# A 32-group attention with an FFN behind it on one core: other filler products on TensorE, later loads for the last batch, and a new table of priorities

## The chip, the cores and the metric

One core of one Trainium2 chip runs the kernel. The metric is the device time of one execution in microseconds; lower is better. TensorE (PE; its weight loads are listed as PEld), VectorE (DVE), ScalarE (ACT), GpSimd (POOL) and SyncE (SP) each work through a list of instructions of their own, in order, and wait for each other through semaphores. POOL and SP also issue the transfers (DMA).

## The reference

Block-sorted attention, and behind it a feed-forward network with a leaky activation:

```python
# q, k, v: (4, 8, 768, 64); sort_net: (4, 8, 8, 8)
for _ in range(5):                          # Sinkhorn
    P = P - max(P, -1); P = exp(P)
    P = P / (sum(P, -1) + 1e-9)
    P = P / (sum(P, -2) + 1e-9)
k_sorted = einsum('bhij,bhjcd->bhicd', P, k_b)   # 8 blocks of 96 rows
v_sorted = einsum('bhij,bhjcd->bhicd', P, v_b)
attn = softmax(q_b @ k_sb.T / sqrt(64))          # inside each block of 96
x = (attn @ v_sb) -> (3072, 512)
h = x @ w_in                                     # 512 -> 2048
out = (max(h, 0) + alpha * min(h, 0)) @ w_out    # 2048 -> 512, float32
```

## The kernel before

The work is cut into 32 groups: group g is block g % 8 of batch g // 8, 96 rows of all 8 heads. `attention(g)` makes the scores (`psS`), their row maximum on VectorE, the exponentials on ScalarE, the product with v (`psO`) and the normalised result `xq`; from group 8 on the weights (`ET`) and the result (`xT`) are turned by DMA transposes that SP issues, before that on TensorE. `ffn1` (line 820) multiplies 2 or 4 groups with 128 columns of w_in into `psH`, and ScalarE (`t`) and VectorE (`hT`) apply the activation; `ffn2` (line 852) multiplies 128 rows with w_out into `psYP` and writes them out.

Ahead of a batch's attention its inputs are prepared. For batch 0 the q loaded at line 423 is turned by `prep_q` (identity products, line 615), k is sorted by `prep_k` (line 615), v is copied into another layout by `conv_v` (ACT, DVE or POOL, line 671) and sorted by `prep_v` (line 682). For batches 2 and 3, `conv_k` (DVE, `KZ<-KS`) and `conv_v` (POOL, 16 copies) lay the data out first, and q comes as eight loads `QN` that six DMA transposes `QTz<-QN` (`turn_q`, line 433) turn; each of these needs all eight loads.

The loads of batch 3 are held back by `paced(g, n)` (line 418): load number n waits for the ET transpose (n even) or the xT transpose (n odd) of group g + n // 2. v starts at g = 9 (line 464), k at 11 (line 452), q at 13 (line 430, two heads for each n).

Every operation is added to a graph with a duration, keys that it reads and writes, and a priority. `plan` (line 205) adds to each priority a shift that two characters of the table `ORDER` give, up to 41 either way (a group counts 1), and `schedule` (line 156) runs the graph in a model of the engines: the operation that can start first goes, by priority among those ready within 60 ns. The result is a fixed list for each engine. In the model, `span` (line 118) counts TensorE's instructions, two for each product, and lets TensorE wait where a count of 256 more is passed sooner than `FETCH_NS` after the last such point (2,500 ns after 36 us); `FETCH0` (line 31) gives the count, the time of the last point and the next threshold to begin with.

`fill` (line 214) then puts extra products into TensorE's list, whose results nobody reads, wherever the model leaves a gap before the first FFN steps. The list begins with 96 products of 16 columns (`short`, line 1006) as soon as the identity matrix is there. A gap that begins before 9 us in the model is filled with bf16 identity products of 512 columns, priced 480 ns each; a later one first with f32 identity products of 512 columns (865 ns) and then with bf16 ones (216 ns), to 0.9 of its length (`warm`, line 998).

## Time and profile before

| | us |
|---|---|
| median of 3 runs | 250.53 (248.55 to 250.69) |
| profiled execution | 250.59 |
| its span, first to last instruction | 248.9 |
| TensorE busy in the span | 231.8 |
| VectorE busy | 177.1 |
| ScalarE busy | 152.2 |
| GpSimd busy | 85.5 |

The profile is one execution. Busy time is the time in which an engine has at least one instruction running; the chain of waits goes back from the last instruction to what released each step. A row of the timeline has start, length, engine, line, operation, output and inputs with their shape, count, and in brackets the idle time before it and what ended it. "issue" is time for which the profile shows no cause.

### The profile page before, as it was taken

The numbers are of one execution on the slowest core, as the hardware profiler recorded it, in microseconds if no ns is written. First come the engines' busy times: TensorE is split into PE (matmuls) and PEld (weight loads), VectorE is DVE, ScalarE is ACT, GpSimd is POOL, SyncE is SP. The second block draws the span as 40 slices with busy tenths as digits, with TensorE's granted clock in tenths as the row PEclk, the third lists the DMA queues.
The fourth block names the chain that finished last, engine by engine and source line by source line (L and its number), as shares of the span: only waits on it lengthen the run. The fifth ranks groups of instructions, "written<-read, shape, count | busy, mean of one in ns | idle before, by whom it ended". The sixth has DMA issues, their size and how long they took to land.

```text
span 248.9 us, 6237 instructions
## 1 busy us (share of the span) xinstructions
PE 231.8 (93%) x2548; PEld 136.3 (55%) x2548; DVE 177.1 (71%) x357; ACT 152.2 (61%) x419; POOL 85.5 (34%) x105
## 2 busy tenths in 40 slices
PE   3997899989889997997999999999999999999995
PEld 3655467667545554554555555555555455555553
DVE  5875497887998969499875668967767877354430
ACT  5564455587966787365875587565775674453441
POOL 8969970089999238995000000000000000000000
PEclk9997999999999999999999999999999999999999
DMA  5999999999699999998445236453334342110112
GB/s 104 202 188 210 208 208 174 210 209 148 82 147 157 185 157 157 161 138 126 34 116 123 37 86 121 84 105 91 87 79 112 60 106 72 47 42 0 43 63 109
DMA packets 66941, 29.79 MB, mean 120 GB/s; under 512 B 58704, under 2 KB 61536, under 8 KB 66912
## 3 DMA queue, kind: packets, MB, share of 16 engines
q0 software_dynamic: 24256, 13.63, 41.0%
q1 hardware_dynamic: 42656, 15.76, 33.9%
q8 instruction: 20, 0.33, 0.5%
q14 instruction: 9, 0.07, 0.1%
HBM read 27.28 MB, written 6.29 MB: 135 GB/s over the span
## 4 chain that ended last, share of the span: by engine, by line
PE 69%; DMA 11%; DVE 8%; POOL 7%; issue 3%; ACT 2%; POOLq 0%; DVEq 0%; SPq 0%
PE psH L830 26%; PE psYP L869 25%; DMA ET<-Esb 6%; DMA VST<-in_v_dram 5%; PE psS L869 3%; PE psO L783 3%; POOL QN L427 3%; POOL VD L397 2%; PE psS L728 2%; DVE KZ L397 2%; DVE hT L843 2%; PE psS L740 1%; DVE xq L793 1%; PE psO L682 1%; DVE nm L734 1%
## 5 line engine op out<-in xcount | busy, mean ns | idle before, releaser
L843 DVE SCALAR_TENSOR_TENSOR hT<-t,omaT,psH 128x384 bf16<-128x384 f32 (+1 forms) x139 | 77.2, 570 | 38.0 <-ACT t L840 36.6
L830 PE MATMUL psH<-xT,w_in_bf 128*128 128x384 bf16 (+1 forms) x556 | 96.9, 311 | 2.9 <-DVE hT L843 2.9
L840 ACT ACTIVATE t<-psH 128x384 f32<-128x384 f32 (+1 forms) x139 | 62.9, 465 | 52.4 <-PE psH L830 47.3
L869 PE MATMUL psYP<-w_out_bf,hT 128*128 128x512 bf16 x336 | 84.6, 379 | 0.0
L830 PEld LDWEIGHTS psH<-xT,w_in_bf 128*128 128x128 bf16 x556 | 49.8, 98 | 36.0 <-DVE hT L843 7.7
L761 ACT ACTIVATE Esb<-psS,nf 96x96 bf16<-96x96 f32 x192 | 46.3, 345 | 1.8 <-DVE nf L734 1.6
L869 PEld LDWEIGHTS psYP<-w_out_bf,hT 128*128 128x128 bf16 x336 | 30.2, 98 | 28.0 <-DVE outstg L397 0.2
L397 POOL COPY VD<-VST 64x384 bf16<-64x384 bf16 (+1 forms) x39 | 34.8, 893 | 19.3 <-DMA VST<-in_v_dram 16.5
L734 DVE TENSOR_REDUCE nf<-psS 96x8 f32<-96x768 f32 x24 | 22.7, 948 | 0.9 <-PE psS L728 0.9
L793 DVE TENSOR_TENSOR xq<-psO,rec 96x512 bf16<-96x512 f32 x31 | 21.2, 685 | 0.9
L427 POOL DMA_DIRECT2D QN<-in_q_dram x24 | 20.7, 877 | 0.0
L397 ACT ACTIVATE VS<-psYP 112x512 bf16<-112x512 f32 x16 | 11.0, 687 | 4.1 <-PE psYP L690 2.7
L790 DVE RECIPROCAL rec<-psO 96x8 f32<-96x8 f32 x31 | 6.2, 200 | 8.3 <-PE psO L783 8.3
L783 PEld LDWEIGHTS psO<-VS,ET 112*128 112x128 bf16 x192 | 8.6, 98 | 6.0 <-DMA ET<-Esb 2.6
L783 PE MATMUL psO<-VS,ET 112*128 112x65 bf16 x192 | 9.9, 194 | 1.6 <-DMA ET<-Esb 1.5
L728 PE MATMUL psS<-KT,QTz 64*128 64x96 bf16 x248 | 10.8, 207 | 0.3 <-ACT Esb L761 0.3
L397 ACT ACTIVATE KT<-psYP 128x512 bf16<-128x512 f32 x11 | 6.6, 597 | 7.2 <-PE psYP L643 4.6
L397 ACT ACTIVATE outstg<-psYP 128x512 f32<-128x512 f32 x12 | 7.2, 597 | 5.7 <-PE psYP L869 5.7
L728 PEld LDWEIGHTS psS<-KT,QTz 64*128 64x128 bf16 x248 | 6.3, 95 | 7.7 <-ACT t L840 3.6
L869 PE MATMUL psS<-w_out_bf,hT 128*128 128x512 bf16 (+1 forms) x48 | 9.3, 344 | 0.0
L397 DVE COPY KZ<-KS 64x1024 bf16<-64x1024 bf16 x12 | 8.4, 710 | 0.1
L397 DVE CAST VS<-psYP 112x512 bf16<-112x512 f32 x10 | 6.8, 683 | 2.3 <-PE psYP L690 2.3
(140 smaller groups left out, 210.1 us busy)
## 6 DMA issues: line engine op xcount, KB each, us to landing
out_dram<-outstg SPq DMA_DIRECT2D x23, 256.0 KB, 2.4
QN<-in_q_dram POOLq DMA_DIRECT2D x24, 96.0 KB, 4.8
w_in_bf<-in_moe_w_in_dram POOLq DMA_DIRECT2D x8, 256.0 KB, 15.9
w_out_bf<-in_moe_w_out_dram POOLq DMA_DIRECT2D x2, 1024.0 KB, 26.4
VST<-in_v_dram POOLq DMA_DIRECT2D x4, 384.0 KB, 19.3
KS<-in_k_dram POOLq DMA_DIRECT2D x2, 768.0 KB, 28.4
KZ<-in_q_dram POOLq DMA_DIRECT2D x1, 768.0 KB, 6.5
KS<-in_k_dram POOLq DMA_DIRECT2D x2, 384.0 KB, 8.8
```

The source lines that it names most:

```text
L397: return e.activation(o, i, ACTF.Copy) if e is nc.scalar else e.tensor_copy(o, i)
L427: G.add(POOL, lambda e, h=h: e.dma_start(AP(QN, h % 4 * 128 + (h // 4) * 64, [[3072, 128], [512, 6], [1, 64]]), AP(q.tensor, b * HB + h * ...
L728: inst = e.matmul(o, AP(QTz[n], hp * 64 * QP + h4 * 768 + i * 96, [[QP, 64], [1, 128]]), AP(KT[n], hp * 64 * ld + (h4 * 8 + i) * bk, [[ld, ...
L734: G.add(DVE, lambda e: e.tensor_reduce(AP(nx, 0, [[8, 96], [4, 2], [1, 4]]), AP(psX, 0, [[1024, 96], [512, 2], [96, 4], [1, 96]]), AxisLis ...
L761: inst = e.activation(AP(Esb[me], p * 128, [[1024, 96], [64, 2], [1, 48]]), AP(psX, (p // 4) * 512 + (p % 4) * 96, [[1024, 96], [48, 2], [ ...
L783: inst = e.matmul(AP(psZ, hp * 512 + h4 * 68, [[1024, 128], [1, 65]]), AP(ET[me] if far else Es0[m], pos(h4, hp) * 96, [[800, nk], [1, 128]]),
L790: G.add(DVE, lambda e: e.reciprocal(AP(rec[m], 0, [[8, 96], [4, 2], [1, 4]]), AP(psZ, 64, [[1024, 96], [512, 2], [68, 4]])), 200, r=banks_ ...
L793: G.add(DVE, lambda e: e.tensor_tensor(out=AP(xq[me], 0, [[512, 96], [256, 2], [64, 4], [1, 64]]), in0=AP(psZ, 0, [[1024, 96], [512, 2], [ ...
L830: inst = e.matmul(AP(pt, poff, [[1024, 128], [1, n]]), AP(w_in_bf, kt * DFF + ft * 128, [[KT_TILES * DFF, 128], [1, 128]]), AP(xT, kt * XR ...
L840: G.add(ACT, lambda e: e.activation(AP(t1[tb], 0, [[384, 128], [1, n]]), AP(pt, poff, [[1024, 128], [1, n]]), ACTF.Relu, scale=-1.0), t_ac ...
L843: G.add(DVE, lambda e: e.scalar_tensor_tensor(out=AP(hT, ft * RING + tok % RING, [[FT_TILES * RING, 128], [1, n]]), in0=AP(t1[tb], 0, [[38 ...
L869: inst = e.matmul(AP(bank[0], bank[1], [[1024, 128], [1, n]]), AP(hT, ft * RING + tok % RING, [[FT_TILES * RING, 128], [1, 128]]), AP(w_ou ...
```

## The change

- The 96 short products are gone. Gaps are filled with bf16 identity products of 512 columns alone, priced 430 ns where the gap begins before 6 us in the model and 216 ns later. The first gap now begins with the identity matrix.
- The loads of batch 3 wait for groups five later: v from group 14, k from 16, q from 18.
- In the planner, `FETCH_NS` is 6000 for 5500, `FETCH0` is (70, -9000, 193) for (205, 6100, 449), and `conv_v` of batches 0 and 1 is priced 580 ns on DVE and 1000 on POOL, for 530 and 870.
- `ORDER` is another table of the same length. The operations and their dependencies are otherwise the same.

```diff
-FETCH_NS = 5500
-FETCH0 = (205, 6100.0, 449)
+FETCH_NS = 6000
+FETCH0 = (70, -9000.0, 193)
 ORDER = (
...
-    def fill(self, make, head, spans):
-
-        out, last = [head], 0.0
-        head.idx = len(self.ops)
-        self.ops.append(head)
+    def fill(self, make, spans):
+
+        out, last = [], 0.0
         for op in self.order["pe"]:
             for lo, hi, deps, bank in spans:
                 begin = max([last, lo] + [self.ops[d].end + 300 for d in deps])
-                left = (op.start - begin) * 0.9
-                n = 0 if begin < 9000 else max(int(left / 865), 0)
-                m = max(int((left - n * 865) / (480 if begin < 9000 else 216)), 0)
-                if op.start <= hi and n + m > 0:
-                    x = _Op("pe", lambda e, n=n, m=m, bank=bank: make(e, n, m, bank), 0, 0.0, None, len(self.ops))
-                    x.start, x.end = begin, begin + n * 865 + m * 216
+                unit = 430 if begin < 6000 else 216
+                m = int((op.start - begin) * 0.9 / unit)
+                if op.start <= hi and m > 0:
+                    x = _Op("pe", lambda e, m=m, bank=bank: make(e, m, bank), 0, 0.0, None, len(self.ops))
+                    x.start, x.end = begin, begin + m * unit
...
-                660, r=paced(13, h // 2) * (b == 3), w=[("QN", h)], prio=prio,
+                660, r=paced(18, h // 2) * (b == 3), w=[("QN", h)], prio=prio,
...
-        load_kv(KS, k, "KS", d_k, 11, b, prio)
+        load_kv(KS, k, "KS", d_k, 16, b, prio)
...
-                load_us / (2 * n), r=paced(9, x) * (b == 3), w=[...],
+                load_us / (2 * n), r=paced(14, x) * (b == 3), w=[...],
...
-        G.add(("act", "dve", "pool"), lambda e: copy(e, o, i), {"act": 872, "dve": 530, "pool": 870},
+        G.add(("act", "dve", "pool"), lambda e: copy(e, o, i), {"act": 872, "dve": 580, "pool": 1000},
...
-    def warm(e, n, m, bank):
+    def warm(e, m, bank):
         t, off, row, keys = bank
         inst = None
-        for x in range(n + m):
-            ident = identf if x < n else identb
-            inst = e.matmul(AP(t, off, [[row, 128], [1, 512]]), ident[:, :], AP(ident, 0, [[128, 128], [0, 4], [1, 128]]))
+        for _ in range(m):
+            inst = e.matmul(AP(t, off, [[row, 128], [1, 512]]), identb[:, :], AP(identb, 0, [[128, 128], [0, 4], [1, 128]]))
         return inst
-
-    def short(e):
-        inst = None
-        for _ in range(96):
-            inst = e.matmul(AP(psYP, 0, [[1024, 32], [1, 16]]), identb[:, :32], identb[:, :16])
-        return inst
-    head = _Op("pe", short, 0, 0.0, None, 0)
-    head.deps.add(ident_op)
-    head.start = G.ops[ident_op].end + 50
-    head.end = head.start + 2700
-
     out1, f1, f2 = warm_at["out"].start, ffn_ops[0].start, ffn_ops[1].start
-    G.fill(warm, head, [(head.end, out1, [ident_op], BANK_Y), (out1 + 1, f1, [warm_at["exp"].idx], BANK_H[0]),
-                        (f1 + 1, f2, [ident_op], BANK_Y)])
+    G.fill(warm, [(0, out1, [ident_op], BANK_Y), (out1 + 1, f1, [warm_at["exp"].idx], BANK_H[0]),
+                  (f1 + 1, f2, [ident_op], BANK_Y)])
```

More of the change, by code (lines that the diff above doesn't have):

```diff
@@ L29 @@
 FETCH = 256
-FETCH_NS = 5500
-FETCH0 = (205, 6100.0, 449)
+FETCH_NS = 6000
+FETCH0 = (70, -9000.0, 193)
 ORDER = (
-    "W0W0W0W0W0W0W0W0W0W0IUW0oNzoJzzqb1-XtR-ce8mk_GX_rIAgo1mHGipMUkZWIcoVY0OLhnmdtdrt-6vnvEh1xPz3QPTopGf_ukhwiQqJnKwQSw_5xq_D"
-    "_4sRWGzyuFs8X0_AvUqVzflHW0jaxEzJzefroGoahWw9O6ozh634KHIjfrDzKWDCBH4SKSXNT2G6YkVZiRZBVAML92wyFpJro3FRLbbWUnOeOXSuHdMdJJSb"
-    "DC8MK3MhIxA9IQEM9DIEThJoHbFruiw6RlkDpkpBb6cWxZlHvSmesYG9upxhPpTyslNVOKSfs6wTcxtNwTyayywCu2kkt1dUIwrLLKp7jJSRtK-6wuyrry-A"
-    "-Lz1yEx6t6v6vgrMv--5wWzzz9tHqBy-_Gv4yrxqzVs-v8ptwLvHx6ajyrVCzfzjtdxPfujnuxOXkMyGej-FcgSsoYnGP-Oyb2qezD-wxdsKiQv_PJr7q_ua"
-    "b6cW3Uh971aX0m0nMaBsOyNe6TOd71Ci9RIfgTE52n101D0m1S22238X3AGq2c7g42JySUEfCxAr7wRkLLFHMW8GPQmQE8O3PQn4AU8sKJ1H8YBTDP1W4pBQ"
-    "SY5x7XJR1V3fZMPxSBQ2Rt6V1LNm161g6R9e40bb9vExHi9NAN69JjKd0m6DIcBZARMe2S2TGOG3W9bQLsZY5mElNJqppuCL4HhdtlKMhBIiRdJA9bXLo2-O"
-    "urKFripmL9DpNwXHwUNKcPU9IK0mmLJRfiGAyGHjJTLCsuQCzXdRtyzn-BzKy_fTxEkHczZznG7vcORodbACZJci1Mkww1iCOlhZZJqepKfki8FHrHAkwHZr"
-    "7wQHBbEDXoxl_5tCZyyEZX_4_GibvLxcaxC2FA0mYcIH3_MgeV8Os3UkaqsiHUtT--lxQasMqzK0G314L7GkCVX_hsSGDpCCC5L7F6TltFjOrrEtqWr_ZV9f"
-    "PMPQjfJEt2gxgiZEw2-DzXulTrKofCPI7XS_TqD4GPVacsGHuNxusAwYoVjABCsbvLwtkzeAzY-6tRfsro-9kl_E1i66yfLKuUkiwMukyuOerOznyvp4lyYn"
-    "b884EKChaEQ8sXgvgMiPqxXPx2nxRmy9aXIB-RcCs0dGnjDfqDKfcHyHsDiy_FnxtdyQg1jG-_ReV2ygUNDQJnQAedRhHQ2ORWY8PtL6C8MAEsGgXUUUa0F8"
-    "d_-cOHVUuZLj_GU5TBFqKARJfHG9E1TbVZijVdFinmj3i_C9yghwp_nwqar8w1ySziwhqTu_rWtFujd0-KfTyKzaA6jrdixDuKurVq_GOPuywwflgJd65Cfj"
-    "Kqt5zSwjqBr-eWc6F-RNJW3wAEQ6apedop-XLe9RYcgBaZZreTsmWmIMMrscC_8b8c1g695ODpiH5n3Lf09tU47wiBbnmpJLHdsUfEXFYbYAVUwJQys3jUWk"
-    "tzo56ymX6-P5IrABr3MFBBKBb7Dyfd7AAxYacctYJh-GYn1xAEprOQ9SXcu2ZdOlG_Az7VfNJ_hg1Dbe5oRtVm2YAOHelyTasRVqj5pfWlUzOYkGQfVsaxYQ"
-    "kb_1tOYuo6WTrHuNIEsyrarmid7e-izWxuSjMShRtPHULZONdbfmao3npqIsSCj0smrvpKuAnRutzyzjmfuYpEbDLx-cjcI4drMUY4ktRmprfDZZpzkLmkTp"
-    "gMkcKoN9Id4ZhGVg7YCvjPvCsIec4t1n5kC29Y5R4K0m105j6FAK0m5pD3YH0mN76c84MnS-STTiry7RNO6ER9PtrQMgYwHPEpSo40LlMWB08XgRnHHYF60r"
-    "qQEWlsaSz8bVWIPhNKHUHQ6I5B3kJnycAJ1OJCCOUV955uWBCaHoIu4rXjBz1ZnVPkocInlvgZkN-LqIx6c8lyw7oSjM_Gyrkfyjwq_GtfqXg-hBxeXFqRml"
-    "4gOYVJCpTGTl1rtnWx3etgK3Cup2a1XVsNLCt9tFv6tr-hpNf7VQfgbztBLhUItcZ1PcM6TQvkZx-VQoMojq_GSuPp_GsBzv_G_6qt_GxPh3-UHV_GOwgkVK"
-    "bcvQvTIFLZ_G-z-I-_ydwhxgdt-CvdsLm1yK_G-F_DtK_D-poH_G_Gvzzqv1YTwrza_G-PwvqNW-k9tNpS-IwH-Oz--Zz1z_zn_8_G_GtAybxUb4-umB-bze"
-    "yr-l_D-z-GvSwbY-wc_G_4-lk7yoqIt5_GzJro-hu3zv_GzJy0uibMmqp4dJZ1sqV3VQN1W7a8fBIEQygTacmjvzogfKO8GIlIVVL8pRiiYJFTR4R3frS2hT"
-    "lcZncMDkftjgIpd6nNt1lliFanmNZzhOvZtSqGPah17qiOc-krhsjSiOval6c_mZq1qeyij2p3lpmxqb5-X9SVMceIgvSGaKIgi3em"
@@ new lines @@
+    "W0W0W0W0W0W0W0W0W0W0EbW0Ud-7z7R0EDpfQhjK1sHyKG8rBn9jsmTKngeHYDY8CgHH7s7Q0u2qBJQA379yA80m4l7V8K1N608IBKNG5v5KGEDFBF1wC0Ga"
+    "19510mDE2EDH8e460m6b3LL96T6x7F419OUmFRQcWzG-AnbK1j9sOV4kPI6VaPW25FEvN8FIGEEa5aOX636J4KDeTU1N0mL_0mV2ZyKGDd0m5_WlDR0mRY4Y"
+    "QCPHLRIAOeX8GcSSJuQleSPM0mTOS0eAfmdGiRe6fTHTkUTcuglAjXVLf3lBexM_ocYdh6w3sShIWal_LJYtONEbl_eRMNXp80SQoif64kGIZxWSaWXcFpUk"
+    "svkVTiaanPdWpj6sG3CgNrTR4KVjKTD0Gc9UojIpiTjXrVkHu-pfLmR3Cu7pM3SpPySHGujKBiFONj91fpr7OEDOtIcCaPp7Siv9u-v3GeFyxOg0PZUZc3uG"
@@ new lines @@
+    "SpIiI9Yp4Nh24yCjEtJawgHG5O4d8wJkCIAAJcmW0mjtQUAa4NB60m0n0m2tNq5aFv83ACWRGBIjFpbLP56e6KGoIg5o1w3R2yN2PBQb8uCKBM9Z6E5r6MKL"
+    "4j2X280m2f0mAF4b2g9w4HOjLs0m5LJf1a2kMJ1mPa4i2o0mEpCo1QcqNp3h1S4nBMH8F1EBW1OzHh8VIF6TF65R2DVRq3AFeI2KEBC-153FHWARpc5nIaBt"
+    "4O5B0n2A3U25GCAAlhI3GL7SmjRnlrZIsdhtSmov_COxnXwrwYs_ipriphlrII8HEYMIibBradguRNqJ7zcgBs5V2H4uJRisBEMKccsHzvSVwj5tBo97hP6q"
+    "8PE8OFHF3wdMcCWOGsFqvHuj_1wNaOfOG9wjbOtuLFbPHAhBSwxaVxQjPzTYL2V0J1eyfeAfAjIRWz_Gwn_GO0zAlF-3f8WSy7o6bmKosWPXXxfPgJEId3GZ"
@@ new lines @@
+    "E_4xRp6zo1NxfVrWv1TSZD2-0u2CCDqiFRFKNKTg6LgxaWWRqhuMZ6-YRJfKRXmYzowFsnYgpzf5CX1bv3JEaXp-hujjmnrTrKKKT-sRXaWQY1rQrqrgtAi-"
+    "s1yzvfsYgIxGq5xkUtlAxerfd7JFYweaq5Xf66b1N6zP9nN3Hitvwtwikst8duvWy9eX2EdqjNpQJ6dwVtOCCS2LL-ZX5gIH1-ZT4oBBxh2oAjENO90my30_"
+    "5g2AKPAG0m9fX2SxB9jEQjIatHcUUme6QeX08g1rIFbcMM5HA41KXxCu1ZOEA6NzmA7afWnD_GifEz_GKQKrrPfZwBhiFmunQGRzD9d6djJiLuViMGUuNqe0"
+    "tmimZTKggwycVroGmH4FhHu5wFZCn5aQHDDcYlPpiDWXSFYjdoMhjhbVUGMDRsjD_0GxIUDZK-FBwUMxU2-DTJ-dyGfZgwlUB0qvwZt9OQHLVlE7MRL3N1ZL"
@@ new lines @@
+    "NpZj1UG-Vq0qWWA_796X3EaP7nBoW8JPcH4rzvhmZdgGCY4JvWdKo8tFDKTUuNdV0mBgsTmNHCXdDvJlWoZ-YROHcpLH0mFrVX6pSrfOsj-nylzfkxA0tbsy"
+    "CmhdO5dDKGSYdXeaycruZepSrHiXwG-S-3zpmLmP-aZ_cW_GlzrrhYoezE_Gi1MtakgFribwgMsZw2-o_GfOL3tiUjSQyKSFuDRVdvV2WswAlw_BqsX2XXc3"
+    "pZi84q5w6luWAdVZqR479OU6HzfuJolGVjaeU2VSMkNs1D22Cy1d7vcDOXDBTWTyRonwfSRXkG0mo81T4M95UsYfyIdHBrCRZwLbZbS132MVU-9oEAkZTScm"
+    "3O8i9qdoJ8341-G95ibQBhBjeJUnfs0x0mGbBARVVNj83kPTSK4u91KcWSJFVFBYp1iSo1IzImuTsbPfD7MR271-aJeVfYngEcLqwuFj9n1C1G69awxnVGVV"
@@ L53 @@
+    "E23tX57E9SDdMnKx8LG03G6F0zAD4bdC0mQOA28AQHSLLnHsUuslK36eFII45DCR1Q0m3UA70m230mBNL1Ez2mI4Jd9l1kIF5z4hGUB_7V3o5wFtCN111HTx"
+    "4KISMD50Jy3Knq69IRAi3P231rE-7NDUJqCxAeaE7vDmNGALGBTYieDEBnD9N8ZJdeZbDVaUBgAlb80mB08BANB-Cd3fBp3dGfVxfc2bQKQN9p5H5UChEERz"
+    "fzUNZ5T10oFjDI2aSX0m6JAZEVLuEalwjLRHghZ5eXuiyarNhwMSlCV4rbitefGOo8jW0tqykFb3hg8-hSgfP5HtcSdBPSDA6KAAA_hfl7shYmpoKoValKdi"
+    "l_8dg1paZD1RXbPlwkm5Yhcsp4qYSZoJrMh4habBcNmChSfGeVkJhulHmjk9sOuNrDr0jFWYrvntxbybvqwMp2yseZu_DWakgvBXZ6"
 )
@@ L463, in load_v @@
                 AP(v.tensor, b * HB + th * 3072 + c * 3072 // n, [[6144, 64], [1, 3072 // n]])),
-                load_us / (2 * n), r=paced(9, x) * (b == 3), w=[("VST", b % 2, y) for y in ((2 * th, 2 * th + 1) if n == 1 else (x,))],
+                load_us / (2 * n), r=paced(14, x) * (b == 3), w=[("VST", b % 2, y) for y in ((2 * th, 2 * th + 1) if n == 1 else (x,))],
                 prio=prio + x / 100, dma=(d_v2[x + 2 * (n - 1)], 0))
```

## Prediction

> **What bounds the kernel now.** I read the page first, then the chain of waits, then the start and the middle by windows and by timeline.

> ```profile
> span 248.9 us, 6237 instructions
> PE 231.8 (93%) x2548; PEld 136.3 (55%) x2548; DVE 177.1 (71%) x357; ACT 152.2 (61%) x419; POOL 85.5 (34%) x105
> 28.00:120.00 92.00, 84.70 (x1107) 52.73 (x1103) 76.89 (x149) 62.99 (x178) 60.98 (x65) 1.00 1.26 160
> 120.00:246.20 126.20, 125.86 (x958) 68.97 (x955) 81.84 (x141) 74.58 (x212) 0.00 (x0) 1.00 0.34 78
> ```

> The last two rows are windows: bounds, length, then busy time and count of PE, PEld, DVE, ACT and POOL, granted clock, DMA share, GB/s. From 120 us to its last product TensorE is idle 126.20 - 125.86 = 0.34 us, so nothing in the order of that stretch can save more than this. In 28 to 120 us it is idle 92.00 - 84.70 = 7.30 us. The rest of what can be won lies ahead of 28 us. The profiled execution took 250.59 us, 1.69 us more than its span, and the median of the runs is 250.53, so the sum is made against 250.59 and needs no correction.

> The chain of waits (start, length, what) names the start and the middle:

> ```profile
> 3.96 12.15 DMA VST<-in_v_dram
> 18.90 1.71 issue
> 26.62 0.70 issue
> 84.16 7.38 DMA ET<-Esb
> 92.79 6.76 DMA ET<-Esb
> ```

> The load of v sets the pace until 16.1 us (3.96 + 12.15). Two stops follow that no engine and no transfer explains ("issue"), 2.41 us together. Later come two slow transposes of the attention weights.

> **What the two stops are.** The PE timeline and windows from zero count products:

> ```profile
> 20.61 0.25 PE L682 MATMUL psO<-BDK,VD 128*64 128x64 bf16 x4 [1.71 <-issue]
> 27.32 0.20 PE L749 MATMUL psH<-QTz,KT 64*128 64x96 bf16 x1 [0.70 <-issue]
> 0.00:6.45 6.45, 2.57 (x96) 2.58 (x96) 3.78 (x28) 3.42 (x9) 5.27 (x14) 1.00 0.61 112
> 0.00:14.00 14.00, 9.96 (x220) 6.90 (x222) 9.95 (x54) 6.78 (x18) 12.82 (x26) 1.00 0.84 159
> 0.00:20.60 20.60, 14.54 (x349) 9.69 (x350) 14.45 (x61) 11.40 (x25) 17.16 (x30) 1.00 0.91 168
> 0.00:23.20 23.20, 17.13 (x414) 11.68 (x416) 15.85 (x64) 12.55 (x27) 19.76 (x34) 0.96 0.94 173
> 0.00:27.30 27.30, 20.55 (x476) 14.03 (x477) 18.42 (x67) 14.28 (x29) 23.86 (x41) 0.94 0.97 178
> q8 instruction: 20, 0.33, 0.5%
> ```

> Each product is two instructions, a weight load and a matmul. The second stop comes 476 - 349 = 127 products, 254 instructions, behind the first. The queue for instructions carried 20 packets, 0.33 MB, for the 5,096 instructions of TensorE in the page's first row: 255 each. I read this so: TensorE's program arrives in blocks of some 256 instructions, 128 products; crossing into a block sends for the next one; and that one is there 6.6 to 6.7 us later (27.32 - 20.61 = 6.71; counting 128 back from 349, product 221 was crossed at 14.0, and 20.61 - 14.0 = 6.6). Whoever uses up 128 products sooner stands still. One block earlier, product 93 was crossed at 6.4 us, among the 96 short products.

> The first stop also costs clock (granted clock is the third figure from the end):

> ```profile
> 21.00:22.00 1.00, 1.00 (x31) 0.77 (x32) 0.59 (x1) 0.30 (x1) 1.00 (x2) 0.64 1.14 211
> 22.00:24.00 2.00, 2.00 (x68) 1.79 (x62) 1.50 (x2) 1.32 (x3) 2.00 (x4) 0.50 1.12 210
> 24.00:25.00 1.00, 1.00 (x25) 0.82 (x22) 0.96 (x4) 0.45 (x1) 1.00 (x3) 0.65 1.15 219
> ```

> Against full clock that is 0.36 + 1.00 + 0.35 = 1.71 us of TensorE time.

> **Part 1: the short products go, gaps hold bf16 products only.**

> ```profile
> 3.88 2.73 PE L1009 MATMUL psYP<-identb 128*32 128x16 bf16 x96 [3.88 <-ACT identb L397]
> 6.54 1.46 PE L1003 MATMUL psYP<-identb 128*128 128x512 bf16 x3
> 7.93 0.63 PE L615 MATMUL psS<-identb,KZ 64*64 64x64 bf16 x16
> 10.63 1.31 PE L1003 MATMUL psYP<-identf 128*128 128x512 f32 x2
> 12.66 1.12 PE L1003 MATMUL psYP<-identf 128*128 128x512 f32 x2
> PEld psYP L615 <- DVE BDK L567: 0.8, 1, 0.8
> ```

> The 96 short products run while TensorE waits for q, whose first product is at 7.93. The gap rule puts (7.9 - 3.9) x 0.9 / 0.43 = 8 wide products there, and with the same rule's start offset 8 or 9; three of them took 1.46 us, 0.49 each, so 8 end near 7.8. Cost 0. Were they all as slow as 0.63, 1.1 us late; even that is covered: the next step on the path, the key products behind the second f32 pair, waits for BDK, the end of the Sinkhorn steps on VectorE (last row), not for q. The four f32 products before 14 us filled 2.43 us; at 0.216 us each bf16 ones are 11, in the same gaps: cost 0, but 7 more products in the count.

> The count is what matters. 99 products before q become about 9, 4 become 11: some 83 fewer. The change's own starting count falls from 205 to 70 instructions, 67 products. I take 75. The first block boundary, product 93, then falls in the q products, 84 of 96 of the way from 7.93 to some 10.7: near 10.0 us. Later blocks open no sooner than 10.0 + 6.6 = 16.6, 23.2 and 29.9. At 23.2 the kernel before has run 414 products, of them 113 fillers (96 short ones, and 17 of L1003 counted in the timeline), 301 useful. The changed one reaches product 349 there, with about 27 fillers: 322 useful. Those 21 products are 0.6 us at the 34 per us of the 22 to 24 us row (x68). The next block lasts until product 477, some 445 useful with 5 more fillers, where the kernel before stood still at 361 (476 less 115 fillers): with 84 more to run before 29.9 the stop of 0.70 has no counterpart. So the first stop moves rather than goes (there will be one just ahead of 23.2, because v lands at 16.1 whatever the order), the second goes: 0.6 + 0.70 = 1.3 us, of which I count 1.2. Bounds: if both stops and the lost clock went, 2.41 + 1.71 = 4.1 us gained; if the new stop is the longer one, 1 us lost (the block opening at 24.2 for 23.2, as a block that took the whole 7.6 us from 6.4 to 14.0, for which nobody waited, would have it).

> [...]

> **Part 2: batch 3 is loaded five groups later.** The values of batch 3 now wait for groups 14 and 15, the keys for 16 and 17, the queries for 18 and 19. In the kernel before they go out from 75.66 us on, just ahead of the two slow ET transposes of the chain: 7.38 and 6.76 us, where the tile's median is 2.9.

> ```profile
> DMA to landing us min/median/max: 2.8/2.9/7.4
> 75.66 0.54 POOL L461 DMA_DIRECT2D VST<-in_v_dram  x1
> 111.65 4.01 DVE L397 COPY KZ<-KS 64x1024 bf16<-64x1024 bf16 x5
> 116.35 1.47 PE L830 MATMUL psH<-xT,w_in_bf 128*128 128x384 bf16 x8 [1.55 <-DVE hT L843]
> PE psO L783 <- DMA ET<-Esb: 1.5, 1, 1.5
> ```

> TensorE stood 1.5 us for the second (until 92.79 + 6.76 = 99.55), and 1.55 us at 116.35 behind key copies of batch 3 on VectorE. Both causes are moved to later: up to 3.05 us. After 120 us TensorE has FFN products in store (0.34 us idle), so the later place should cover the same delays. New waits of this kind and the new order take some back; I count half, 1.5 us. Bounds: 3.05 gained, 0 gained, and the rival below.

> The queues: on GpSimd the 16 copies of v for batch 3 and the loads behind them now stand behind waits for groups 14 to 19; GpSimd has no work after 120 us (0.00 busy), so there is room. On SP, the transposes of q stand ahead of ET, xT and the output writes; see the slow rival.

> **Part 3: planner constants and the new order.** Copies of v are now priced 580 and 1000 ns, a block 6000. The rows have 647 and 1038, and 6.6 us.

> ```profile
> L397 POOL COPY VD<-VST 128x384 bf16<-128x384 bf16 x7 | 7.3, 1038 | 16.8 <-DMA VST<-in_v_dram 16.5
> L397 DVE COPY VD<-VST 128x384 bf16<-128x384 bf16 x5 | 3.2, 647 | 0.4 <-DMA VST<-in_v_dram 0.4
> ```

> All three move towards what the chip did, so the plan should fit a little better; I give it no term. The order itself can't be read from its table. It can at best take the 7.30 us of idle time in 28 to 120, and could add as much.

> Sum: 250.6 - 1.2 - 1.5 = 247.9.

> **Rivals.** (a) Forecast, 247.9, own range 245.5 to 249.5. (b) No change, near 250.3: the moved first stop is as long and as cold as the old one, and the new order loses in the middle what the loads gain; within it, that the stops belong to the work and not to the count, so that the head gives nothing: 250.6 - 1.5 = 249.1. Against it stand the 127 products between the stops. [...] (c) Slower: batch 3 comes too late.

> ```profile
> 116.12 1.19 SPq L435 DMA_TRANSPOSE QTz<-QN  x1
> 140.90 1.18 SPq L801 DMA_TRANSPOSE xT<-xq  x1
> 164.31 1.21 SPq L766 DMA_TRANSPOSE ET<-Esb  x1
> 202.61 1.22 SPq L766 DMA_TRANSPOSE ET<-Esb  x1
> xT<-xq SPq DMA_TRANSPOSE x24, 2.4
> QN<-in_q_dram POOLq DMA_DIRECT2D x24, 96.0 KB, 4.8
> QTz<-QN SPq DMA_TRANSPOSE x18, 5.0
> ```

> Batch 3's first QTz transpose goes at 116.12 now. Changed, it needs the xT of group 19 (issued 140.90, 2.4 to land), a load (4.8) and itself (5.0): 153 us, against group 24's ET at 164.31: 11 us of room, less the scores and exponentials ahead of that ET. Five more QTz transposes follow, on the one SP queue on which ET and xT stand behind them. If batch 2 runs 8 to 11 us later than now, or SP stands in front of a late load, batch 3 slides: groups 24 to 31 take (202.61 - 164.31) / 7 = 5.5 us each, and one group lost, less what the FFN store covers, is 3 to 5 us: 253.6 to 255.6. It decides from the point where the first QTz of batch 3 lands after group 24's scores are due, a few us ahead of 164.

> **How the numbers follow.** Chances: (a) 0.42, (b) 0.32, (c) 0.26. About 1%, 2.5 us, is what a measurement of this kernel tells from no change: faster means below 248.0, slower above 253.0. Of (a) three quarters lie below 248.0 (0.32), a quarter above (0.10); of (b) 0.05 below, as far as both gains come in full, 0.26 within, 0.01 above; (c) is above. Together 0.37, 0.36, 0.27. The range goes from 245.0, past the low end of (a), to 254.0, which takes in (b) and a part of (c).

> **What would show it.** Right: no stop of TensorE before product 349 and one just ahead of 23 us; none near 27; ET of groups 12 to 15 landing in under 5 us; no wait of 1.5 us at those two places. Wrong: a stop at the fourth v unit as before, more than 7.3 us idle between 28 and 120, or TensorE idle after 140 us waiting for QTz, ET or xT of batch 3.

## The result and the profile after

The changed kernel takes 248.22 us (median of 20 runs, 246.79 to 250.67), the kernel before 250.74 us (20 runs, 248.55 to 253.99). The ratio is 0.991, 95% interval 0.989 to 0.994: about 2.2 us faster, 0.9%. Ratios, here and below, leave out the executions that took over 1.5% longer than the fastest of their kernel, so they can differ a little from the quotient of two medians. The profiled execution took 247.19 us with a span of 245.5; against the profiled execution before (250.59, 248.9) that is 3.4 us. It is the third fastest of the 20, so this pair lies about 1 us further apart than the two kernels do, and what is split up below is the pair. The forecast was 247.9; by the bound of 1% set there the result lies just inside no change.

The page of the changed kernel (line numbers are 3 to 4 lower than before):

```profile
span 245.5 us, 6074 instructions
PE 230.0 (94%) x2463; PEld 133.3 (54%) x2463; DVE 175.7 (72%) x357; ACT 153.0 (62%) x420; POOL 83.9 (34%) x104
q8 instruction: 19, 0.31, 0.5%
```

TensorE runs 2,463 products where it ran 2,548, and is idle for 15.5 us (245.5 - 230.0) where it was for 17.1. The queue for instructions carried 19 packets for 20. The PE timeline of the start, with the windows row that counts products to the first stop:

```profile
3.86 4.02 PE L999 MATMUL psYP<-identb 128*128 128x512 bf16 x9 [3.86 <-ACT identb L394]
22.05 0.21 PE L746 MATMUL psS<-QTz,KT 64*128 64x96 bf16 x1
22.90 0.33 PE L746 MATMUL psS<-QTz,KT 64*128 64x96 bf16 x7 [0.64 <-issue]
28.21 0.50 PE L827 MATMUL psH<-xT,w_in_bf 128*128 128x192 bf16 x4
0.00:22.20 22.20, 15.03 (x349) 8.68 (x350) 16.73 (x64) 12.76 (x28) 18.93 (x34) 1.00 0.92 168
```

And the first FFN product of the kernel before:

```profile
31.24 0.50 PE L830 MATMUL psH<-xT,w_in_bf 128*128 128x192 bf16 x4
```

The stop of 1.71 us in the v products and that of 0.70 near 27 us are gone. One stop of 0.64 us stands exactly behind product 349, and the block opens at 22.90 us. The granted clock stays at full speed there (1.00 from 22.9 to 28.2 us), and the first FFN product starts 3.03 us sooner (28.21 for 31.24). But little of this lead is left at 60 us. The rows below show a second stop and the scores of group 8, the first group of batch 1; then the chain of waits up to those scores; then TensorE's work from 60 us on in both kernels, the changed one first:

```profile
47.13 0.26 PE L805 MATMUL psO<-identb,xq 96*128 96x96 bf16 x2 [0.72 <-issue]
60.45 0.34 PE L725 MATMUL psS<-KT,QTz 64*128 64x96 bf16 x8 [0.74 <-DMA QTz<-QN]
```

```profile
23.74 23.10 DMA QN<-in_q_dram
46.86 13.54 DMA QTz<-QN
```

```profile
60.00:247.00 187.00, 179.56 (x1532) 100.37 (x1532) 130.41 (x229) 117.66 (x344) 42.20 (x50) 1.00 0.66 99
```

```profile
60.00:247.00 187.00, 179.91 (x1540) 100.41 (x1536) 133.00 (x231) 117.58 (x345) 43.98 (x53) 1.00 0.62 98
```

At 60 us the changed kernel has only 179.91 - 179.56 = 0.35 us less TensorE work ahead of it. q of batch 1 lands near 46.9 us, its transposes end at 60.4 (46.86 + 13.54), and group 8's scores wait for them, however early the head was done. Ahead of that a new stop of 0.72 us, behind 729 recorded products (the count of blocks puts it at 733), and a stretch at half clock from 49.2 to 52.6 us, worth 1.7 us of TensorE's time, took most of what the head had gained. Without them TensorE would have waited longer for q: after_again below is such an execution.

Most of the gain comes from 80 to 120 us. Windows before, and after (second figure: length, third: TensorE busy):

```profile
60.00:80.00 20.00, 17.90 (x236) 10.74 (x233) 18.16 (x35) 15.19 (x55) 19.19 (x22) 1.00 1.30 133
80.00:100.00 20.00, 17.69 (x210) 10.63 (x209) 17.29 (x31) 15.83 (x48) 9.82 (x15) 1.00 1.22 161
100.00:120.00 20.00, 18.45 (x141) 10.07 (x139) 15.70 (x25) 11.59 (x32) 14.97 (x18) 1.00 1.04 126
```

```profile
60.00:80.00 20.00, 17.90 (x214) 10.55 (x214) 16.26 (x31) 14.79 (x49) 19.24 (x22) 1.00 1.84 156
80.00:100.00 20.00, 18.94 (x236) 11.64 (x234) 18.23 (x32) 16.12 (x50) 0.76 (x1) 1.00 0.55 100
100.00:120.00 20.00, 19.93 (x141) 10.50 (x138) 15.35 (x28) 11.43 (x33) 10.29 (x14) 1.00 1.58 153
```

Idle time falls from 2.31 to 1.06 us in 80 to 100 and from 1.55 to 0.07 in 100 to 120 us: 2.73 us. With 0.35 from the head and 0.32 behind 120 us (idle 0.34 there before, 0.02 after) that is the 3.4 us between the two spans. The ET transposes issued between 81 and 100 us, before and after (the tile's row):

```profile
DMA to landing us min/median/max: 2.9/6.1/7.4
```

```profile
DMA to landing us min/median/max: 2.9/3.2/4.5
```

Their median falls from 6.1 to 3.2 us. No load of batch 3 is under way there any more. GpSimd's rows after, with those loads:

```profile
48.34 2.15 POOL L442 DMA_DIRECT2D KS<-in_k_dram  x4 [12.59 <-PE psYP L612]
102.25 0.54 POOL L458 DMA_DIRECT2D VST<-in_v_dram  x1 [21.49 <-DMA ET<-Esb]
103.09 6.59 POOL L424 DMA_DIRECT2D QN<-in_q_dram  x8 [0.31 <-issue]
117.81 0.52 POOL L458 DMA_DIRECT2D VST<-in_v_dram  x1 [4.87 <-DMA xT<-xq]
```

Only v is loaded later: from 102 to 118 us, where it went out from 75.7 to 88.8. k goes out at 48 us, earlier than before (82 to 103), and q from 103 us, nearly as before (from 101): it stands behind the first v load in GpSimd's list. The code says why: the waits are looked up among operations that are in the graph already (`if k in self.last_w`), and the loads of batch 3 enter it behind group 15. A wait for groups 16 to 19 therefore isn't there. For k (16, 17) and q (18, 19) the change took the wait away. The text above the prediction, and the prediction, say that they wait for those groups; that is wrong.

What looks like the same delay is left at another place of the changed kernel: its chain of waits runs through an ET transpose issued at 71.93 us that takes 7.86 us, while q of batch 2, sent out from 66.9 to 74.4 us, is loaded, and TensorE waits 0.60 us for it.

### The profile page after: what moved, and what is told of

It is laid out like the page before. It is cut to its first block, busy times and chain, and to the rows that moved or that the text cites. A ratio compares the mean times of both kernels' runs of the same rounds, so it can differ in the third digit from the quotient of the medians.

```text
span 245.5 us, 6074 instructions
## 1 busy us (share of the span) xinstructions
PE 230.0 (94%) x2463; PEld 133.3 (54%) x2463; DVE 175.7 (72%) x357; ACT 153.0 (62%) x420; POOL 83.9 (34%) x104
## 4 chain that ended last, share of the span: by engine, by line
PE 65%; DMA 23%; DVE 4%; POOL 4%; ACT 1%; issue 1%; POOLq 0%
PE psH L827 29%; PE psYP L866 25%; DMA QN<-in_q_dram 9%; DMA QTz<-QN 6%; DMA VST<-in_v_dram 5%; PE psS L866 4%; DMA ET<-Esb 3%; PE psS L725 2%; PE psO L780 2%; POOL QN L424 2%; PE psYP L687 1%; DVE hT L840 1%; PE psYP L640 1%; DVE VS L394 1%; POOL VD L394 1%
## 5 line engine op out<-in xcount | busy, mean ns | idle before, releaser
L827 PE MATMUL psH<-xT,w_in_bf 128*128 128x384 bf16 (+1 forms) x556 | 98.1, 312 | 0.7 <-DVE hT L840 0.3
L866 PEld LDWEIGHTS psYP<-w_out_bf,hT 128*128 128x128 bf16 x336 | 30.8, 98 | 29.3 <-DVE outstg L394 0.4
L394 POOL COPY VD<-VST 64x384 bf16<-64x384 bf16 (+1 forms) x38 | 33.5, 883 | 6.0 <-DMA VST<-in_v_dram 1.9
L394 ACT ACTIVATE outstg<-psYP 128x512 f32<-128x512 f32 x14 | 8.4, 597 | 10.7 <-PE psYP L866 10.5
L999 PE MATMUL psYP<-identb 128*128 128x512 bf16 x36 | 11.2, 443 | 3.9 <-ACT identb L394 3.9
L458 POOL DMA_DIRECT2D VST<-in_v_dram x6 | 3.4, 572 | 28.5 <-DMA ET<-Esb 21.5
```

Of the source, the lines that this page charges most:

```text
L394: return e.activation(o, i, ACTF.Copy) if e is nc.scalar else e.tensor_copy(o, i)
L827: inst = e.matmul(AP(pt, poff, [[1024, 128], [1, n]]), AP(w_in_bf, kt * DFF + ft * 128, [[KT_TILES * DFF, 128], [1, 128]]), AP(xT, kt * XR ...
L866: inst = e.matmul(AP(bank[0], bank[1], [[1024, 128], [1, n]]), AP(hT, ft * RING + tok % RING, [[FT_TILES * RING, 128], [1, 128]]), AP(w_ou ...
L999: inst = e.matmul(AP(t, off, [[row, 128], [1, 512]]), identb[:, :], AP(identb, 0, [[128, 128], [0, 4], [1, 128]]))
```

## Experiments

Names with a_ start from the changed kernel, those with b_ from the kernel before. Each ratio is to the kernel before, run beside it.

**The count of products, and nothing else.** a_short96, a_short40 and a_short64 put 96, 40 or 64 short products back ahead of the list; all lists stay, the gaps are filled behind them.

```diff
-        out, last = [], 0.0
+        out, last = [head], 0.0
...
+        for _ in range(96):
+            inst = e.matmul(AP(psYP, 0, [[1024, 32], [1, 16]]), identb[:, :32], identb[:, :16])
```

> The changed kernel with the 96 products of 16 columns put back ahead of everything (lists otherwise the same, gaps filled behind them). Theory, blocks of 128 products that open 6.7 us after the one before is entered: product 93 falls into the short products again (6.4 us), product 349 now stands in the third v unit and opens near 20.4 us, product 477 stands in the second group's score step and opens near 27.1 us, so a stop of some 3.9 us there (from about 23.2), with the clock at half behind it. First FFN product near 31.5 to 32 us for 28.2 in the changed kernel. If the lead of the head counts at the end, time 249.7 to 251.5 us (ratio to the kernel before 0.996 to 1.003); if it is lost on the way anyhow, 248.2 (0.990). Rival, stops belong to the work: stops at 22 and 46 us as in the changed kernel, first FFN product at 28.2, ratio 0.990.

PE timeline of a_short96:

```profile
21.82 0.51 PE L681 MATMUL psO<-BDK,VD 128*64 128x64 bf16 x13 [1.27 <-issue]
28.09 0.34 PE L748 MATMUL psH<-QTz,KT 64*128 64x96 bf16 x7 [1.58 <-issue]
33.22 0.50 PE L829 MATMUL psH<-xT,w_in_bf 128*128 128x192 bf16 x4
```

Product 349, counted in its list, stands in the v products and product 477 is the first of the second group's score step; it stopped at both, for 1.27 and 1.58 us. The places were forecast; the blocks opened later (21.8 and 28.1 for 20.4 and 27.1), the second stop was 1.58 us where 3.9 were expected, since TensorE came later, and the first FFN product came 5.0 us behind the changed kernel's, beyond the forecast 3.3 to 3.8. Its four runs (249.06 to 255.37 us, median 253.81) scatter too much for a ratio.

> The changed kernel with 40 short products ahead in place of 96. Block theory: product 349 stands in the fifth or sixth v unit, opens near 21.9 us, a stop of about 0.9 us; product 477 stands in the first FFN products, opens near 28.6, a stop of 1 to 1.5 us; first FFN product behind 29 us, between the changed kernel (28.2) and the one with 96. Time between both, ratio 0.990 to 0.998. Rival, stops belong to the work: no change against the changed kernel, stops at 22.3 and 46.4.

The first profile of a_short40, and that of a second set (a_short40_again):

```profile
22.10 0.38 PE L681 MATMUL psO<-BDK,VD 128*64 128x64 bf16 x13 [0.34 <-issue]
28.20 0.50 PE L829 MATMUL psH<-xT,w_in_bf 128*128 128x192 bf16 x4
60.52 0.34 PE L727 MATMUL psS<-KT,QTz 64*128 64x96 bf16 x8 [2.21 <-DMA QTz<-QN]
```

```profile
23.15 0.53 PE L681 MATMUL psO<-BDK,VD 128*64 128x64 bf16 x13 [2.00 <-issue]
31.70 0.50 PE L829 MATMUL psH<-xT,w_in_bf 128*128 128x192 bf16 x4
```

The stop stands at the same product both times (13 products of the row are left), but it lasts 0.34 us once and 2.00 us the other time: the block opened 1.05 us later (23.15 for 22.10), and TensorE came 0.6 us sooner (21.15 for 21.76). The expected second stop behind 27 us was absent: TensorE came to product 477 only at 28.3 us, and by then the block was there, at most 6.2 us behind the opening of the one before. The two heads differ by 3.5 us (28.20 and 31.70), the two executions by 1.3 us (246.69 and 247.97). Most of the difference goes into the wait for batch 1's q: 2.21 us at 60.52 in the first, 0.32 at 61.42 in the second. 247.28 us, ratio 0.987 (0.981 to 0.993).

> The kernel before without its 96 short products (order, f32 fillers, loads and constants as before). Block theory: the stop of 1.71 us in the fourth v unit goes; product 349 is now the last v product and opens near 23.3 us, so a stop of 0.5 to 2 us ahead of that; none near 27 us; first FFN product near 29 us for 31.2. Time 1 to 2.5 us less, ratio 0.990 to 0.996, if the lead is kept; 1.000 if later stops give it back. Rival, stops belong to the work: stops at 18.9 and 26.6 as before, ratio 1.000.

```diff
-        out, last = [head], 0.0
+        out, last = [], 0.0
```

```profile
23.69 0.22 PE L680 MATMUL psO<-BDK,VD 128*64 128x64 bf16 x2 [2.12 <-issue]
31.25 0.50 PE L828 MATMUL psH<-xT,w_in_bf 128*128 128x192 bf16 x4
```

The stop moved to the last v products, as the count has it (2 of the unit are left), and none was left near 27. But the block opened only at 23.69, the stop took 2.12 us and the clock fell behind it (0.50 from 26 to 28 us): the first FFN product is where it was (31.25 for 31.24). That step of the expectation failed. The ratio is 0.993 (0.988 to 0.998) all the same; what made those 0.7% the trace doesn't settle.

The traces also hold the packets of the instruction queue, 16,384 bytes each, with their times. In all 14 traces, TensorE makes 20 stops of 0.3 us or more ahead of 70 us for which the timeline shows no other cause, and each of them ends 1.26 to 1.59 us behind the end of such a packet: packets end at 19.35 and 25.84 us in the kernel before (stops end at 20.61 and 27.32), at 21.43 and 45.63 in the changed one (22.90 and 47.13). I read these stops as waits for TensorE's program to arrive. What isn't constant is the time from crossing into a block to the opening of the next: 6.6 and 6.7 us in the kernel before, 6.3 between the two stops of a_short96, 4.8 ahead of the changed kernel's first stop (product 221 was crossed at 18.06 us), 8.4 ahead of the stop of 2.00 us in a_short40_again.

**The new table of priorities.** a_oldorder is the changed kernel with the old table, b_neworder the kernel before with the new one; nothing else is exchanged.

> The changed kernel with the table of priorities of the kernel before; fillers, constants and loads are the changed ones. If the new table makes the gain of the middle (idle TensorE in 60 to 120 us 6.0 us before, 3.2 changed), idle there goes back to 5 us or more and the ratio is 0.997 or above; if the loads make it, idle stays near 3 and the ratio near 0.990. Head as in the changed kernel either way: first FFN product at 28 to 29.5 us.

> The kernel before with the new table of priorities alone; fillers, constants and loads as before. If the new table is better by itself, idle TensorE in 60 to 120 us falls from 6.0 towards 3 us and the ratio is 0.98 to 0.99. If a table fits only the constants and waits with which it was made, as the old table under the changed constants (ratio 1.035) suggests, the time is 253 to 260 us, ratio 1.01 to 1.04.

a_oldorder took 259.15 us, ratio 1.035 (1.028 to 1.041); b_neworder 271.73 us, ratio 1.087 (1.083 to 1.092). Neither table is better by itself: each fits the constants and waits with which it was made, and under others it gives a worse plan. In a_oldorder TensorE idled 5.9 us between 60 and 120 us and 6.2 between 120 and 236, where the changed kernel has 3.2 and next to nothing; its first FFN product came at 30.60 us and not at 28 to 29.5. In b_neworder the idle time from 60 to 120 us rose to 10.0 us. (b_neworder runs the work in another order with the fillers of the kernel before, and it too stops at 350 and 477 recorded products.) This rules out neither the loads nor the table as the cause of the middle, since both were re-planned. The next two runs leave the plan alone.

**When v and k are loaded, with the lists fixed.** In a_vfree the four v loads lose their waits after the planning and move ahead of the q loads in GpSimd's list; in a_kvback the k loads also move there, with the old waits for groups 11 and 12.

```diff
     total = G.plan(ORDER)
+    vs = G.ops[613:617]
+    for op in vs:
+        op.deps -= gates
...
+    G.order["pool"] = lst
```

> The changed kernel with all its lists as they are, but the four v loads of batch 3 no longer wait for groups 14 and 15 and stand ahead of the q loads in GpSimd's list: they go out near 81 us in place of 102 to 118, as in the kernel before. If the later v makes the gain of the middle, ET, xT and QTz transposes of 83 to 99 us land in 5 us or more (3 in the changed kernel), TensorE idles 4.5 us or more between 60 and 120 us (3.2) and the time is 249 to 250 us, ratio 0.994 to 0.998. Rival, the loads don't matter: 0.990.

GpSimd, then TensorE, then the row of the ET transposes issued between 81 and 100 us, all of a_vfree:

```profile
81.76 2.11 POOL L458 DMA_DIRECT2D VST<-in_v_dram  x4
```

```profile
61.28 0.38 PE L725 MATMUL psS<-KT,QTz 64*128 64x96 bf16 x8 [3.06 <-DMA QTz<-QN]
93.21 0.62 PE L780 MATMUL psO<-VS,ET 112*128 112x65 bf16 x8 [5.09 <-DMA ET<-Esb]
```

```profile
DMA to landing us min/median/max: 2.8/6.9/10.3
```

With v in flight the three ET transposes land in 6.9 us at the median (3.2 for four in the changed kernel), the longest in 10.3, and TensorE waits 5.09 us for one of them. The wait of 3.06 us at 61.28 lies ahead of the moved loads and isn't theirs. 251.68 us, ratio 1.006 (1.002 to 1.010), against 0.991: this edit alone costs 1.5%, more than the whole gain of the change, and at least twice what was expected. (This profiled execution took 255.45 us; the size is taken from the ratio, the profile only shows where.)

> As the one with v early, and the four k loads of batch 3 taken from 48 us to behind v, each waiting for group 11 or 12 as in the kernel before: k and v together load in some 81 to 97 us. If these loads cost the kernel before its idle time in the middle, idle in 60 to 120 us is 5 to 6 us and the time 249.5 to 251 us, ratio 0.995 to 1.000. Rival, the new table alone makes the middle: idle stays at 3.2 and the ratio at 0.990.

The four runs took 255.5 to 262.25 us, median 260.77, too scattered for a ratio but all above the kernel before, and far above the expected 249.5 to 251. PE and then DVE rows of the profiled execution (262.25 us):

```profile
91.76 0.62 PE L780 MATMUL psO<-VS,ET 112*128 112x65 bf16 x8 [6.07 <-DMA ET<-Esb]
112.42 2.74 PE L827 MATMUL psH<-xT,w_in_bf 128*128 128x384 bf16 x8 [5.31 <-DVE hT L840]
109.90 0.86 DVE L394 COPY KZ<-KS 64x1024 bf16<-64x1024 bf16 x2 [5.82 <-DMA KS<-in_k_dram]
```

The first wait, 6.07 us for ET, is that of a_vfree again: the first k load went out only at 92.11 us, when it was over. The second, 5.31 us, is another: the key copies waited for the last k load, which went out at 105.75 us, and what VectorE does for the FFN stood behind them. So this run repeats the cost of v and adds that of k come late; it doesn't show that k loads beside the transposes slow them. The next run looks at that.

> The changed kernel with its lists, but the four k loads of batch 3 taken from 48 us, where they run beside the six QTz transposes of batch 1, to behind the v copies of batch 2, waiting for groups 10 and 11 (about 80 to 92 us). Theory: batch 1's q, landed at 60.4 us in nearly every run, sets when group 8 starts and takes up whatever the head gained; without k beside them the first QTz lands 1.5 to 2 us sooner, group 8's ET is issued near 62.9 for 64.7, and 0.5 to 1.5 us stay at the end, ratio 0.984 to 0.988. Rival: the k loads now slow the ET and xT transposes of 83 to 97 us, as early v did, TensorE waits 1 us or more for ET there and the ratio is 0.992 to 1.005.

a_kpaced moves only k, with waits for groups 10 and 11. SP, then TensorE:

```profile
62.16 1.21 SPq L763 DMA_TRANSPOSE ET<-Esb  x1
```

```profile
93.35 0.54 PE L780 MATMUL psO<-VS,ET 112*128 112x65 bf16 x8 [3.18 <-DMA ET<-Esb]
```

Both theories show in this trace. Without k beside them the six QTz transposes of batch 1 land in 8.4 us at the median, as in the kernel before, where the changed kernel has 10.7; group 8's ET goes out at 62.16 us for 64.73, and no wait for QTz is left. But the k loads now slow the transposes behind 80 us, and TensorE waits 4.0 us for ET in all, 3.18 at 93.35: gained at 60 us, lost at 93. The time is 247.82 us, ratio 0.991 (0.988 to 0.994). The profiled execution is the longest of the eight (250.99 us), so how much the others lose at 93 us isn't shown.

**Loads that are really late.** a_late gives k and q the waits that the text of the change names; the planner makes new lists.

```diff
+    for op, key in late:
+        op.deps.add(G.last_w[key])
     total = G.plan(ORDER)
```

> The changed kernel with the waits of k and q that its text names made real: in the changed kernel the waits for groups 16 to 19 do not exist, because the loads enter the graph behind group 15, so k goes out at 48 us and q at 103. Here k waits for 16 and 17, q for 18 and 19; the planner makes new lists with the same table. By the slow rival of the prediction the QTz transposes of batch 3 come 25 to 30 us later (from 123 to about 150 us) and push batch 3's groups: TensorE idle after 140 us, time 251 to 255 us, ratio 1.00 to 1.02. If the room holds: 0.990.

```profile
154.23 4.60 SPq L436 DMA_TRANSPOSE QTz<-QN  x3
```

262.36 us, ratio 1.048 (1.041 to 1.054). Batch 3's first QTz goes at 154.23 us (123.35 in the changed kernel); TensorE is busy 14.56 of the 20 us from 160 to 180 and 16.35 of those from 180 to 200. The cost is far above the expected 3 to 5 us; how much of it is the lateness and how much the re-made plan under a table that doesn't fit, this run can't tell.

**The changed kernel and two counts side by side.**

> The changed kernel as it is, beside the two others of this set on the same chip, for the comparison. Ratio near 0.991 as before; head with one stop of 0.6 us at 22 and one of 0.7 us at 46, first FFN product at 28.2.

> The changed kernel with 40 short products, once more, for its time against the changed kernel's. The block theory says: no stop at 46 us and none above 0.4 us ahead of it, as in its first profile, so also fewer half-clock stretches; 1 us less than the changed kernel, ratio 0.987 to the kernel before. Rival: the first set's 247.28 was scatter, and both are at 0.991.

> The changed kernel with 64 short products. Block theory, with the arrival times of the profile with 40: product 477 now comes 24 useful products sooner, is reached near 27 us less the wait, and opens near 28.4: a stop of about 1.6 us there, and about 0.2 us near 22; first FFN product 1.5 to 2.5 us behind 28.2, and half clock behind the stop. Ratio 0.993 to 1.000. Rival, only many short products hurt (their own 1.8 us on TensorE): no stop at 477, ratio as with 40.

after_again 248.37 us, ratio 0.990 (0.986 to 0.994); a_short40_again 247.19, 0.986 (0.982 to 0.991); a_short64 247.10, 0.985 (0.980 to 0.990). PE timeline of a_short64, then of after_again:

```profile
27.02 0.20 PE L782 MATMUL psYP<-VS,Es 112*128 112x65 bf16 x1 [0.67 <-issue]
29.18 0.50 PE L829 MATMUL psH<-xT,w_in_bf 128*128 128x192 bf16 x4
60.69 0.34 PE L727 MATMUL psS<-KT,QTz 64*128 64x96 bf16 x8 [2.08 <-DMA QTz<-QN]
```

```profile
22.93 0.33 PE L746 MATMUL psS<-QTz,KT 64*128 64x96 bf16 x7 [0.46 <-issue]
60.80 0.34 PE L725 MATMUL psS<-KT,QTz 64*128 64x96 bf16 x8 [2.08 <-DMA QTz<-QN]
```

a_short64 stops at its product 477 near 27 us, for 0.67 us where 1.6 was expected; the half clock came ahead of that stop (20.0 to 23.4 us) and not behind it. Its head is 1 us later than the changed kernel's; it is not slower for that. In after_again the stop at 46 us is absent (its packet ends at 44.77 us, in the first profile at 45.63), no clock is lost ahead of 60 us (1.00 from 28 to 60), and instead TensorE waits 2.08 us for QTz, where the first profile had 0.74, and runs at half clock behind that wait (61.9 to 65.4 us): whoever comes early waits. Both counts read 1.2 us below the changed kernel in this set, and the first set of 40 had a ratio of 0.987; the intervals overlap, and no place in the traces accounts for it. They have the lowest ratios measured, but that they beat the changed kernel isn't shown.

## Why the prediction came out right, and where its steps failed

- **The time was within the range, but the range was wide.** 245.0 to 254.0 us holds the kernel before too (250.74), so that 248.22 lies in it says little; the steps say more.
- **The blocks of 128 products: right in the place, lucky in the time.** Product 349 stopped where it was put (322 useful products done), and the stop near 27 us went. Four other counts, and another order with the old count, put the stops within two products of where the count has them, so the rival that the stops belong to the work is out. The block opened at 22.90 us for 23.2 forecast, but not by the forecast's sum of 10.0 + 6.6 + 6.6: product 221 was crossed at 18.06 us and not at 16.6, and the next block was there 4.84 us later and not 6.6. By the rule of 6.6 it would have opened at 24.7, the stop would have been 2.4 us, and the 0.6 us of the sum would have gone. Not foreseen: a later block, near product 733, stopped TensorE for 0.72 us at 46.4 us, 6.7 us behind the crossing of the block before.
- **The head's 1.2 us: wrong in two ways.** At the first FFN product the lead was 3.03 us, since the stop was short and did not cost the clock. But the step "second goes: 0.6 + 0.70" took that lead to the end, and it isn't kept: 0.35 us were left at 60 us. What the working missed is q of batch 1, which landed at 60.4 to 60.8 us in the changed kernel, after_again, a_short40 and a_short64, with TensorE waiting 0.7 to 2.2 us for it. The k loads that now run beside its transposes are part of that (a_kpaced).
- **The middle's 1.5 us: the mechanism right, the size too small, a premise wrong.** Slow ET transposes beside the loads of batch 3, and waits behind them, are what went: 2.73 us of idle time, of the 3.05 that I had as the bound. a_vfree shows the cause for v in the changed kernel, with all lists but GpSimd's fixed. That v costs the kernel before just as much is argued from the same rows; the kernel before with a later v was not run. That k and q go later as well was wrong, and with it the reading of the key copies: they run at 97 to 107 us now, earlier than before (109 to 116), not later.
- **The sum came close because two errors met:** in the profiled pair the head gave 0.85 us less than forecast and the middle 1.23 more; with 0.32 behind 120 us that is 3.4 us for 2.7. Between the kernels themselves it is 2.2 us, and no run splits that up. b_noshort alone has 0.7% of the 0.9 with no gain at the first FFN product, so how much is the loads' and how much that of the missing short products stays open.
- **The slow rival:** its mechanism needed a wait that the changed kernel doesn't have. Where it was made, QTz came at 154 us for the 153 worked out, and the price was 262 us for 254 to 256.
- **The clock:** the half-clock stretches come and go from run to run. In the changed kernel's 20 runs a lower mean granted clock goes with a longer time: 1.000 in 3 runs with a mean of 247.35 us, 0.992 or 0.993 in 11 with 248.04, below that in 6 with 249.48. Stops of 1.27 us (a_short96) and 1.71 us (the kernel before) cost the clock here, while one of 0.64 us (the changed kernel) cost nothing. In the traces of all 14 executions a half-clock stretch inside TensorE's work lasts 3.41 or 6.83 us, and starts a whole number of 3.41 us behind the first change to full clock. In 19 of the 20 falls from full clock TensorE was idle 1.58 us or more, in sum, in the 3.41 us just ahead; three such stretches of 1.58 us or more (1.68 to 1.78) cost nothing. So in these traces the falls go with the idle sum of such a stretch more than with the length of one stop. The one fall that doesn't fit (1.05 us idle ahead of it) is in these rows of the changed kernel. From the end of the stop at 46 us they show the clock falling some 2 us behind a stop of only 0.72 us, with 0.33 us more idle in between (granted clock third from the end):

```profile
48.00:49.00 1.00, 0.67 (x19) 0.47 (x17) 0.97 (x3) 0.60 (x1) 0.66 (x2) 1.00 0.99 203
49.00:50.00 1.00, 1.00 (x16) 0.98 (x13) 0.82 (x2) 0.30 (x1) 1.00 (x3) 0.60 1.04 215
51.00:52.00 1.00, 1.00 (x17) 0.67 (x16) 0.60 (x3) 0.70 (x3) 0.94 (x2) 0.50 1.06 216
52.00:53.00 1.00, 1.00 (x9) 0.44 (x6) 1.00 (x3) 1.00 (x2) 0.94 (x2) 0.69 1.12 223
```

## What to carry to other kernels

A lead won at the start is worth only what is left at the next arrival that doesn't depend on it (here 0.35 us at 60 us, of 3.03 at the first FFN product): look for that arrival in the chain of waits before counting the lead to the end. Keep bulk loads out of the stretch in which DMA transposes are on the critical path; four loads of 192 KB, sent out at 82 to 84 us in place of 102 to 118 with every other engine's list fixed, cost 1.5% here. And check that a wait that a change names exists in the graph, and that a tuned table of priorities is not carried to other constants: here that cost 3.5 and 8.7%.
